# Nineteen constant matmuls ahead of the first transposes, and the fifth projected tile taken out of PSUM by VectorE

## The chip, the cores and the metric

The kernel runs on one core of a Trainium2 chip. The metric is the device time of one execution in microseconds (us). TensorE multiplies matrices into PSUM; VectorE (DVE in the profile), ScalarE (ACT) and GpSimd (POOL) do the elementwise work and take results out of PSUM; SyncE (SP) issues the DMAs.

## The reference

The input is x, 2048 tokens of 512 numbers. With xn = layernorm(x), the result is x + s * g, where s is a dilated local attention and g a gated MLP, both on xn:

```python
def _A_ref(x, wqkv, wo):              # H = 32 heads of 16, W = 8 neighbours, dilation 2
    q, k, v = (x @ wqkv) split into heads
    idx = pos[:, None] - arange(8)[None, :] * 2          # positions before 0 are masked
    attn = softmax(einsum("bhsd,bhswd->bhsw", q, k[idx]) * Dh ** -0.5)
    o = einsum("bhsw,bhswd->bhsd", attn, v[idx])
    return o @ wo
def _B_ref(x, w1, b1, w2, b2):        # 512 -> 1376 -> 512
    y = layernorm(x)
    return gelu(y @ w1 + b1) @ w2 + b2
xn = layernorm(x)
return x + _A_ref(xn, wqkv, wo) * silu(_B_ref(xn, w1, b1, w2, b2))
```

## The kernel before

The tokens are split by parity into two halves of 1024 (c = 0 and 1, since the dilation is 2), each in eight tiles of 128 tokens; the heads are split into four blocks of 128 columns. A "unit" is one half with one block of heads: eight units in all. For each unit `qkv` multiplies the eight normalised and transposed tiles (`yT`) with that block's q, k and v weights (`wq`), twelve matmuls to a tile: all operands are kept as a high and a low float16 part, so a product is high x high, low x high and high x low, four matmuls of 384 columns each. The tile stands in one PSUM buffer of the rings `ps` and `mh` and is then scaled by a per-token factor (`cs`) and written to `U`, by ScalarE (line 824) or by VectorE (line 820). Copies on SP shift the keys and values of the neighbours into place ("halo", line 832), and VectorE does the attention of the unit. The MLP runs over four chunks of 512 tokens and eleven slices of the hidden layer (`mlp1`, line 1111; `mlp2`, line 1158), and the output projection is line 1025.

The first unit (u = 0) stands at the start, while inputs still arrive. `ln0` normalises the tiles in the order 2, 3, 0, 1, 4, 5, 6, 7 (IORD0): statistics (lines 661, 662) and small factors (625, 647) on VectorE, a power on GpSimd (635), the normalised tile on VectorE (697, or 730 in two parts for tile 2, or 665 on ScalarE for tile 4), four transposes on TensorE (704; 738 for tile 2), then the high part by ScalarE (719) and the low part by VectorE (720). Tiles 2 and 3 go another way in this unit: their transposed tile is copied to `L` (741, 708) and multiplied in float32 with the unscaled weights (809). Meanwhile `prep_q` finds the scale of the weights: a sum of squares on ScalarE (578), a sum over the partitions by a matmul with a constant tile `fours` (495, one for each half of the weights), a few tiny steps on VectorE (506, 513, 519, 524), then the high part of the weights by ScalarE (600, four pieces) and the low part by VectorE (602, four pieces). Line 500 is the same sum for the other weights. The last four of a tile's twelve matmuls in this unit read the low parts of the weights, each its own piece, and each waits for that piece of line 602.

Which tile of a unit VectorE takes out of PSUM is listed in `EDVE`, for the first and the second unit; the others go to ScalarE.

The order on each engine is written by a planner (class `Plan`). Every operation has an estimated duration, a priority and its dependencies; `order` places them one after another by estimated time, and each engine then runs its list in that order, without reordering. `place` estimates DMAs from a rate and a start; `SEEDS` perturbs the estimated durations before the order is made, so other seeds give another order throughout the kernel. "Constant matmuls" are matmuls of `fours` with itself into a buffer that nobody reads (line 1260). Their priority of 1e9 lets them be placed only where nothing else is ready by the planner's estimate; before, thirty have no dependency at all, and four more wait for the normalised tile 2.

```python
EDVE = ((5, 6, 7), ())
...
    idle = fours
    for n in range(WAKE0 + WAKE):
```

Of the kernel before, what the change touches and what calls it, by code (L numbers as in the profile page):

```python
# [19 lines left out]
P = 128  # L20
# [34 lines left out]
W2LATE = 4  # L55

QDVE = ()
EDVE = ((5, 6, 7), ())

BEFORE_W1 = (0, 1, 4, 5)  # L60

# [34 lines left out]
class Plan:  # L96
# [71 lines left out]
    def start(self):  # L168
        for o in self.ops:
            o.npred, o.ready, o.succs = len(o.preds), 0.0, []  # L170
        for o in self.ops:
            for p in o.preds:
                p.succs.append(o)
        self.free = {o.eng: 0.0 for o in self.ops}
        self.portfree, self.dma, self.landed, self.table = 0.0, 0.0, [], None
        self.held = False

    def earliest(self, o):
# [7 lines left out]
    def place(self, o, t):  # L186

        if o.eng == "sp":
            if not o.nbytes:
                return t  # L190
            self.free["sp"] = t + o.issue
            self.dma = max(self.dma, t + o.issue + 0.3)
            self.dma += o.nbytes / (o.rate if self.dma > SLOW else 265e3)
            end = self.dma + o.tail
            self.landed.append(end)
            return end
        end = t + o.dur
        if o.nbytes:
            self.free[o.eng] = end
            self.dma = max(self.dma, end + 0.3) + o.nbytes / o.rate  # L200
            return self.dma + o.tail
        if o.eng == "act" and o.table is not None and o.table != self.table:
            end += 1.3
            self.table = o.table
        if o.hold is not None:
            self.held = o.hold
        self.free[o.eng] = end
        if o.port:

            self.portfree = end - (0.25 if o.eng == "pool" else 0.0)  # L210
        return end + LAT[o.eng]
# [123 lines left out]
    def issue(self):  # L335
        self.lengths = [(o.dur, o.tail, o.rate) for o in self.ops]
        best = min(SEEDS, key=lambda seeds: self.judge(seeds)[0]) if len(SEEDS) > 1 else SEEDS[0]
        order = self.judge(best, 0)[1]
# [3 lines left out]

SEEDS = ((186, 978148, 510074, 22688, 804624, 962081, 422754, 653699, 424371, 432252),)

LAT = {"dve": 0.12, "act": 0.14, "pool": 0.07, "pe": 0.06}
MARGIN = {"pe": 0.2, "dve": 0.15, "act": 0.05}  # L350

SLOW = 5.5

QUEUE = 8

# [3 lines left out]

PTOT = 0.5  # L360

WAKE = 4
WAKE0 = 30
PS1 = 0.72

QHI = 4
# [25 lines left out]
def tile_mixer(ctx, tc, a_x, a_wqkv, a_wo, b_w1, b_b1, b_w2, out):  # L392
    nc = tc.nc
    pl = Plan()
# [384 lines left out]
    def qkv(c, hb, u):  # L779
# [11 lines left out]
        left = pl.users([(x, ub, j) for x in "qkv" for j in range(NI)])  # L791
        on_dve = EDVE[u] if u < 2 else ()
        for n, i in enumerate(IORD if u else IORD0):
# [461 lines left out]
    zero_halo(0)  # L1255
    zero_halo(1)
    idle = fours
    for n in range(WAKE0 + WAKE):
        b = R_z[0].new()
        pl.add("pe", 0.2 if n < 16 else 0.1, lambda b=b: nc.tensor.matmul(b.t[:, 0:2 * P], idle[:, 0:P], idle, start=True,  # L1260
                                                       stop=True), [("yd", 2)] if n >= WAKE0 else [], [b], prio=1e9)
    pl.prio = 0.6
    qkv(0, 0, 0)
    pl.prio = PWQ1
# [196 lines left out]
```

## Time and profile before

| | |
|---|---|
| median of 3 runs | 413.49 us (413.47 to 413.73) |
| the profiled execution: its own time | 413.5 us |
| its span, first to last instruction | 411.7 us |
| instructions | 5576 |

A page of the profile shows one execution. Its parts are the busy time of each engine, the span in 40 slices, the DMA queues, the chain of work that ended last (followed back from the last instruction to what released it), the costliest groups of instructions, and the DMA issues. A timeline row gives start and length in us, engine, line, operation, what is written and read, the shape, how often (x), and in brackets the idle time before it and what ended it. Lengths of matmuls are modelled and overlap the next; their pitch is read from start to start.

### The profile page before, as it was taken

The page shows a single profiled execution, that of the slowest core. Times are in us where ns is not written, and L with a number is a line of the kernel's source. Part 1 is how long each engine was busy: PE and PEld are TensorE (multiplying, and loading weights), DVE is VectorE, ACT ScalarE, POOL GpSimd, SP SyncE. Part 2 cuts the span into 40 slices and gives each one's busy share as a digit, 9 for nine tenths or more (in the row PEclk, how much of TensorE's full clock was granted, in tenths as well). Part 3 has the DMA queues.
Part 4 walks back from the last instruction along what each step waited for, and adds up shares of the span by engine and source line. Part 5 has one row for each costly group of instructions (what it writes and reads, how often), then busy time and mean ns, then how long its engine had stood idle before and what let it go on. Part 6 is the DMA issues. An engine that isn't in the chain of part 4 may idle for free.

```text
span 411.7 us, 5576 instructions
## 1 busy us (share of the span) xinstructions
PE 407.0 (99%) x2098; PEld 208.8 (51%) x2098; DVE 387.3 (94%) x372; ACT 224.5 (55%) x359; POOL 114.2 (28%) x160
## 2 busy tenths in 40 slices
PE   8999999999999999999999999999999999999996
PEld 6666444446544554456444644445655554444443
DVE  5999999999999999999999979999989999999965
ACT  4999999876569377432675261126311492234500
POOL 7620542052912250015101500054036500250022
PEclk9999999999999999999999999999999999999999
DMA  8963350500343448400740070302063367008034
GB/s 291 415 259 90 98 198 0 204 2 1 90 111 120 105 128 160 81 0 2 175 144 27 2 164 27 104 0 74 4 192 112 102 205 156 2 0 256 2 79 176
DMA packets 42666, 44.83 MB, mean 109 GB/s; under 512 B 27496, under 2 KB 27936, under 8 KB 42128
## 3 DMA queue, kind: packets, MB, share of 16 engines
q1 hardware_dynamic: 42640, 44.49, 36.4%
q8 instruction: 16, 0.26, 0.2%
q14 instruction: 10, 0.08, 0.1%
HBM read 23.53 MB, written 7.34 MB: 75 GB/s over the span
## 4 chain that ended last, share of the span: by engine, by line
PE 99%; DVE 0%; issue 0%
PE z L1158 28%; PE ps L802 27%; PE mh L1111 26%; PE ps L1025 6%; PE mh L802 2%; PE z L1025 2%; PE z L1260 1%; PE mh L1025 1%; PE ps L1111 1%; PE z L704 1%; PE mh L809 1%; PE ps L809 1%; PE z L738 0%; DVE U L1081 0%; DVE U L1084 0%; PE mh L1142 0%
## 5 line engine op out<-in xcount | busy, mean ns | idle before, releaser
L1111 PE MATMUL mh<-yT,w 128*128 128x512 f16 (+1 forms) x504 | 115.5, 379 | 0.0
L802 PE MATMUL ps<-wq,yT 128*128 128x384 f16 x684 | 114.5, 326 | 0.0
L1158 PE MATMUL z<-w,h 128*128 128x512 f16 x480 | 111.0, 379 | 0.0
L802 PEld LDWEIGHTS <-yT 128*128 128x128 f16 x744 | 72.4, 98 | 48.6 <-issue 0.2
L1111 PEld LDWEIGHTS <-w 128*128 128x128 f16 (+1 forms) x528 | 52.9, 100 | 60.9
L1128 ACT ACTIVATE mh<-mh,b1T,hsc 128x512 f32<-128x512 f32 (+1 forms) x42 | 31.5, 749 | 85.1 <-PE mh L1111 84.8
L1158 PEld LDWEIGHTS <-h 128*128 128x128 f16 x480 | 46.9, 98 | 55.7
L872 DVE TENSOR_TENSOR prod<-U 128x2048 f32<-128x2048 f32 x32 | 72.9, 2282 | 1.4 <-DMA U<-U 1.0
L876 DVE TENSOR_REDUCE L<-prod 128x128 f32<-128x2048 f32 x32 | 73.1, 2285 | 0.8
L824 ACT ACTIVATE U<-ps,cs 128x384 f32<-128x384 f32 x57 | 32.9, 579 | 60.4 <-PE ps L802 58.5
L945 DVE TENSOR_TENSOR prod<-L,U 128x2048 f32<-128x2048 f32 x25 | 60.1, 2423 | 0.2
L976 POOL COPY gate<-prod 1x1 f32<-1x1 f32 x24 | 4.2, 173 | 157.6 <-DVE prod L872 157.6
L977 POOL TENSOR_TENSOR prod<-prod 128x1024 f32<-128x1024 f32 x14 | 32.9, 2349 | 0.0
L1025 PEld LDWEIGHTS <-oT 128*128 128x128 f16 x204 | 19.8, 98 | 21.7
L936 DVE TENSOR_TENSOR prod<-prod,prod 128x2048 f32<-128x2048 f32 x13 | 29.7, 2283 | 0.0
L1025 PE MATMUL ps<-wo,oT 128*128 128x512 f16 (+1 forms) x132 | 28.5, 367 | 0.0
L1136 DVE SCALAR_TENSOR_TENSOR h<-mh,hsc,h 128x512 f16<-128x512 f32 x36 | 26.4, 735 | 0.6 <-ACT h L1132 0.6
L1132 ACT ACTIVATE h<-mh,hsc 128x512 f16<-128x512 f32 x38 | 26.0, 683 | 0.8
L977 POOL TENSOR_TENSOR prod<-prod,oT 128x1024 f32<-128x1024 f32 x3 | 10.0, 3324 | 41.7 <-DVE prod L936 41.7
L1018 POOL TENSOR_TENSOR f<-f,f 128x512 f32<-128x512 f32 x4 | 10.6, 2639 | 22.6 <-DMA U<-U 18.9
L977 POOL TENSOR_TENSOR prod<-prod,prod 128x1024 f32<-128x1024 f32 x7 | 16.4, 2350 | 0.0
L1018 POOL TENSOR_TENSOR U<-U,f 128x512 f32<-128x512 f32 x4 | 5.5, 1374 | 34.3 <-DVE U L1090 34.3
(184 smaller groups left out, 411.1 us busy)
## 6 DMA issues: line engine op xcount, KB each, us to landing
f<-in_A_x_dram SPq DMA_DIRECT2D x31, 256.0 KB, 3.3
U<-U SPq DMA_DIRECT2D x16, 392.0 KB, 4.1
gd<-f SPq DMA_DIRECT2D x12, 256.0 KB, 2.8
oT<-in_B_w_dram SPq DMA_DIRECT2D x2, 1024.0 KB, 9.1
yT<-in_B_w_dram SPq DMA_DIRECT2D x2, 1024.0 KB
f<-gd SPq DMA_DIRECT2D x8, 256.0 KB, 3.8
out_dram<-f SPq DMA_DIRECT2D x8, 256.0 KB, 3.0
out_dram<-U SPq DMA_DIRECT2D x7, 256.0 KB, 2.0
```

The source lines that it names most:

```text
L802: nc.tensor.matmul(b.t[:, 0:384], y[:, s, k, o:o + P], wq[:, hb, t, k], start=(n == 0), stop=(n == 11))
L824: act(384, lambda i=i, b=b: nc.scalar.activation(U3[:, i:i + 31:15, :], b.t[:, 0:384].rearrange("p (t e) -> p t e", t=3), AF.Identity, sca ...
L872: first = dve(2048, lambda p2=p2, g=g: nc.vector.tensor_tensor(p2(), q, slots(Ut, KH, 2 * g), op=ALU.mult), qk + [("kh", ub, 0), ("kh", ub ...
L876: first.then = dve(2048, lambda pr=pr, g=g: nc.vector.tensor_reduce(L3()[:, 2 * g:2 * g + 2], pr.t.rearrange("p (r f d) -> p r f d", r=2, ...
L936: dve(n, lambda: nc.vector.tensor_tensor(d(), a(), b(), op=ALU.add), keys, [dkey])
L945: dve(2048, lambda: nc.vector.tensor_tensor(dst().rearrange("p (r f d) -> p r f d", r=2, d=DH), L3()[:, 2 * g:2 * g + 2].rearrange("p r (f ...
L977: nc.gpsimd.tensor_tensor(d, d, y(), op=ALU.add)
L1025: nc.tensor.matmul(b.t[:, cols], oT[:, hb, i // 4, s, i % 4], wo[:, t, hb, cols], start=(hb == 0 and n == 0), stop=(hb == last and n == 2))
L1111: nc.tensor.matmul(b.t[0:M], w1[:, s, k, f * P:f * P + M], yT[ch][:, t, k], start=(n == 0), stop=(n == 11))
L1128: act(512, lambda: nc.scalar.activation(b.t[0:M], b.t[0:M], AF.Gelu_apprx_tanh, bias=b1T[0:M, f:f + 1], scale=hsc[0:M, 1:2]), [b, ("b1T",) ...
L1136: dve(512, lambda: nc.vector.scalar_tensor_tensor(lo()[0:M], b.t[0:M], hsc[0:M, 2:3], hi()[0:M], op0=ALU.mult, op1=ALU.subtract), [b, hk], ...
L1158: nc.tensor.matmul(z.t, hl[s][0:K, t * P:(t + 1) * P], w2[0:K, w, f], start=(f == 0 and n == 0), stop=(f == NF - 1 and n == 2))
```

## The change

The constant matmuls become nineteen, none of which waits for anything. The first has priority 0 and an estimate of 1.333 us, the others 0.153 us each at the old priority. VectorE takes tiles 4, 6 and 7 of the first unit out of PSUM, in place of 5, 6 and 7. The planner's estimate of the DMAs starts at 2.24 us and has no slower first stretch, and the seeds are others.

```diff
-EDVE = ((5, 6, 7), ())
+EDVE = ((4, 6, 7), ())
...
-        self.portfree, self.dma, self.landed, self.table = 0.0, 0.0, [], None
+        self.portfree, self.dma, self.landed, self.table = 0.0, FIRST, [], None
...
-            self.dma += o.nbytes / (o.rate if self.dma > SLOW else 265e3)
+            self.dma += o.nbytes / o.rate
...
-SEEDS = ((186, 978148, ...),)
+SEEDS = ((500165, 389854, ...),)
...
-SLOW = 5.5
+FIRST = 2.24
...
-WAKE = 4
-WAKE0 = 30
+WAKE = 19
...
-    for n in range(WAKE0 + WAKE):
+    for n in range(WAKE):
         b = R_z[0].new()
-        pl.add("pe", 0.2 if n < 16 else 0.1, lambda b=b: nc.tensor.matmul(b.t[:, 0:2 * P], idle[:, 0:P], idle, start=True,
-                                                       stop=True), [("yd", 2)] if n >= WAKE0 else [], [b], prio=1e9)
+        pl.add("pe", 0.153 + (1.18 if n == 0 else 0.0), lambda b=b: nc.tensor.matmul(
+            b.t[:, 0:2 * P], idle[:, 0:P], idle, start=True, stop=True), [], [b], prio=1e9 if n else 0.0)
```

In the order that the planner then writes, the engines' lists differ in these places (lines as before the change). TensorE: nineteen constant matmuls in place of 23 at the start, and none of the two, two and five that stood further on in the first unit, nor of the two behind the last product; the first transpose of line 738 stands ahead of the first sum of line 495, and the second sum of line 495 ahead of the first transposes of line 704. Later, one group of three of line 1111 and six of line 1158 trade places with their neighbours. VectorE: line 820 for tile 4 stands where one line 720 stood, one line 647 two places further up, and two pairs of neighbours later on are swapped. ScalarE: line 824 for tile 5 in place of the one for tile 4; around the first MLP steps line 1128 and line 542 trade places; a SiLU (line 1174) joins the three ahead of it, which saves two loads of a function table. GpSimd: one pair swapped. SP: three pairs of neighbours swapped. The instructions are otherwise the same.

More of the change, by code (lines that the diff above doesn't have):

```diff
@@ L341, in issue @@
             o.fn()
-SEEDS = ((186, 978148, 510074, 22688, 804624, 962081, 422754, 653699, 424371, 432252),)
+SEEDS = ((500165, 389854, 427978, 647943, 394648, 289068, 629827, 866434, 58414, 290909, 969430, 478841,
+          326988, 34468, 300308, 816254, 306888, 41293, 60788, 308971, 890734, 237800, 376148, 36800, 231455,
+          772755, 355690, 761464),)
 LAT = {"dve": 0.12, "act": 0.14, "pool": 0.07, "pe": 0.06}
 MARGIN = {"pe": 0.2, "dve": 0.15, "act": 0.05}
-SLOW = 5.5
+FIRST = 2.24
 QUEUE = 8
```

## The prediction

> **What bounds the kernel now.** I read the page first, then the timeline of TensorE over the first 30 us, then VectorE and ScalarE over the same stretch, and last a few places late in the run where the new order moves something.
>
> The page:
> ```profile
> span 411.7 us, 5576 instructions
> PE 407.0 (99%) x2098; PEld 208.8 (51%) x2098; DVE 387.3 (94%) x372; ACT 224.5 (55%) x359; POOL 114.2 (28%) x160
> PE 99%; DVE 0%; issue 0%
> ```
> The chain that ended last is TensorE from end to end. Its useful work is the same before and after, so only two things can move the time: constant matmuls that stand between useful ones, and stalls. The first 24 us of TensorE (start, length, line, count; a length is modelled and overlaps the next row, so I read the pitch from start to start):
> ```profile
> 1.18 5.09 PE L1260 MATMUL z<-fours 128*128 128x256 bf16 x23 [1.18 <-DVE s L1315]
> 6.06 0.21 PE L495 MATMUL z<-s,fours 128*128 128x1 bf16 x1
> 6.13 1.08 PE L738 MATMUL z<-ident,f 128*128 128x128 f32 x4
> 7.02 2.18 PE L809 MATMUL ps<-prod,L 128*128 128x384 f32 x6
> 9.03 0.60 PE L704 MATMUL z<-ident,f 128*128 128x128 f32 x4
> 9.47 0.17 PE L495 MATMUL z<-s,fours 128*128 128x1 bf16 x1
> ...
> 13.43 0.38 PE L1260 MATMUL z<-fours 128*128 128x256 bf16 x2
> 13.65 0.60 PE L704 MATMUL z<-ident,f 128*128 128x128 f32 x4
> 14.09 0.81 PE L802 MATMUL ps<-wq,yT 128*128 128x384 f16 x4
> 14.73 0.38 PE L1260 MATMUL z<-fours 128*128 128x256 bf16 x2
> 14.95 0.81 PE L802 MATMUL mh<-wq,yT 128*128 128x384 f16 x4
> ...
> 17.78 0.71 PE L1260 MATMUL z<-fours 128*128 128x256 bf16 x5
> 18.32 0.81 PE L802 MATMUL ps<-wq,yT 128*128 128x384 f16 x4
> 18.97 0.81 PE L802 MATMUL mh<-wq,yT 128*128 128x384 f16 x4
> 19.62 2.11 PE L802 MATMUL ps<-wq,yT 128*128 128x384 f16 x12
> 21.57 0.60 PE L704 MATMUL z<-ident,f 128*128 128x128 f32 x4
> ...
> 23.98 0.60 PE L704 MATMUL z<-ident,f 128*128 128x128 f32 x4
> ```
> Two things are to be seen. The opening 23 constant matmuls have a pitch of (6.06-1.18)/23 = 0.212 us, the five at 17.78 one of 0.108: TensorE runs at half speed at first. The four transposes of 6.13 still take 0.22 each, the six passes of 7.02 take 0.335, so full speed comes at about 7.2. (The page's granted clock shows full speed throughout; this slowness is in the pitch alone.) And from 13.43 on, rows follow each other without a hole: TensorE works on, also through the nine constant matmuls at 13.43, 14.73 and 17.78, which take 9 x 0.108 = 0.98 us of the path.
>
> Who would be late without them? VectorE and ScalarE there:
> ```profile
> 5.34 0.34 DVE L730 TENSOR_SCALAR f<-prod,lw,lw 128x128 f32<-128x128 f32 x1 [0.69 <-POOL lw L635]
> 6.32 0.69 DVE L661 BATCH_NORM_STATS2 bn<-prod 128x6 f32<-128x512 f32 x1 [0.24 <-DMA prod<-in_A_x_dram]
> 8.10 0.55 DVE L697 TENSOR_SCALAR f<-prod,lw,lw 128x512 f32<-128x512 f32 x1 [0.63 <-POOL lw L635]
> 9.51 0.15 DVE L625 TENSOR_SCALAR lw<-lw 128x1 f32<-128x1 f32 x1
> 9.71 0.16 DVE L506 TENSOR_SCALAR ssq<-z 128x1 f32<-128x1 f32 x1
> 14.22 1.38 DVE L720 TENSOR_TENSOR yT<-z,yT 128x512 f16<-128x512 f32 x2
> 16.04 2.20 DVE L602 SCALAR_TENSOR_TENSOR wq<-prod,qsc,wq 128x384 f16<-128x384 f32 x4
> 19.16 1.28 DVE L720 TENSOR_TENSOR yT<-z,yT 128x512 f16<-128x512 f32 x2
> 23.09 0.54 DVE L697 TENSOR_SCALAR f<-prod,lw,lw 128x512 f32<-128x512 f32 x1
> 14.29 0.58 ACT L719 CAST yT<-z 128x512 f16<-128x512 f32 x1
> ```
> After the wait at 8.10 VectorE shows none up to 25 us. Its start is held by a DMA (6.32) and GpSimd (8.10), neither of which the change touches, so VectorE's chain is what limits how much of the 0.98 us comes back.
>
> **The change part by part.**
>
> *Four of the opening 23 go, and the first transpose passes ahead of L495.* The 19 that are left end at 1.18 + 19 x 0.212 = 5.21. The first quarter of the normalised tile is there at 5.34 + 0.34 = 5.68, so the first transpose runs at about 5.74, not 6.13. The other three need the rest of that tile; at L697's 0.55 us for 512 columns its 384 take about 0.41, so they run from about 6.13, as the first did before, and with 3 x 0.212 L809 starts at 6.77, not 7.02. Of these 0.25 us the half speed until 7.2 takes half: L809 ends at 8.9, not 9.03.
>
> *L495 ahead of L704.* L495 now runs at 8.9, not 9.47. L506 on VectorE waited for it: it stood at 9.71, while L625 at 9.51 allows 9.58. VectorE gains 0.13 us.
>
> *The nine in between go.* L704 at 13.65 moves up by 0.1 from the start and 0.22 from its two constant matmuls, to 13.33; its input is ready before that. The products of 14.95 need the cast of 14.29, which ends at 14.87; as the cast itself waits for L704, but also for ScalarE's work before it, I give it 0.2: they start at 14.70. The 2.83 us of work from 14.95 to 17.78 then end at 17.53. Next come four products that each wait for one of the four L602. That quartet ends at 16.04 + 2.20 = 18.24; it gains the 0.13, and 0.10 more because the pair of L720 at 14.22 has in it 0.10 that the like pair at 19.16 has not (a wait for that same cast), and the new order puts a 0.07 us step there. So the last L602 ends at 18.01, the fourth product runs at 18.06 and ends at 18.22, in place of 18.97: 0.75 us ahead. With two groups of 0.65 (18.32 to 18.97, and the like) tile 4's first third then ends at 19.52, but its second third needs the first L720 of 19.16, which ends at 19.84 - 0.23 = 19.61: a stall of 0.14. Lead: 0.61 us. That wait is what comes late next.
>
> *VectorE takes tile 4 out of PSUM, ScalarE tile 5.* One L820 of 0.61 us stands earlier on VectorE, and one L720 of a tile that is not wanted yet moves behind L697 in exchange: the transposes of 23.98 need the L697 of 23.09 (ends 23.63, new 23.4), and would start at 23.37. That is even, to 0.05. ScalarE's 0.6 us only move by a few places; neither buffer is written again before the next unit, so I cost it at nothing. Cover gone, it would be 0.05 to 0.1.
>
> *The rest of the order.* The new seeds and DMA start move seven groups on TensorE, all of the same work. On SP's queue three pairs of neighbours change places, among them a halo copy that now stands behind a store and waits for its SiLU; the reader of that copy is several of VectorE's 2.3 us instructions further on. On GpSimd two short steps swap. Both cost nothing under that cover. Two places on TensorE are tight. First, at 215 us four products move ahead of a 2.6 us block, and their buffer must have been read by a SiLU that now comes directly behind the other three, into an output buffer that a store still reads:
> ```profile
> 211.05 6.11 SPq L1177 DMA_DIRECT2D gd<-f  x4
> DMA to landing us min/median/max: 2.0/2.8/3.1
> 215.20 2.75 PE L1111 MATMUL mh<-yT,w 128*128 128x512 f16 x12
> ```
> The store issued at 211.05 lands at 213.05 to 214.15, the SiLU of 0.69 ends by 214.9, before 215.2: no stall, and two table loads of 1.28 us on ScalarE vanish beside TensorE. Second:
> ```profile
> 331.36 1.04 ACT L824 ACTIVATE U<-ps,cs 128x384 f32<-128x384 f32 x2
> 331.99 2.11 PE L802 MATMUL ps<-wq,yT 128*128 128x384 f16 x12
> ```
> Here L802 starts as soon as ScalarE has emptied its buffer (331.36 + 0.58), so a lead of TensorE lasts only if the others have it too. They have:
> ```profile
> 29.86 0.16 DVE L504 TENSOR_REDUCE s<-z 128x1 f32<-128x4 f32 x1 [0.20 <-PE z L500]
> 249.13 0.75 DVE L1039 SCALAR_TENSOR_TENSOR f<-ps,osc,f 128x512 f32<-128x512 f32 x1 [0.25 <-PE ps L1025]
> ```
> VectorE waited for TensorE at 29.86 and at 249.13, so it takes over the lead. The two constant matmuls at the end of TensorE's list stand behind the last useful one and cost nothing now.
>
> *Sum.* The profiled execution took 413.5 us for a span of 411.7; the median of the runs is 413.49, so I take them as one. 413.5 - 0.6 = **412.9 us**. A measurement of this kernel can tell about 0.2% (0.83 us) from no change, so this counts as within it.
>
> **The rivals.**
>
> *Slower: full speed comes late.* Before, it took 6.0 us of unbroken matmuls (1.18 to 7.2). After, TensorE stands still from 5.21 to 5.74 and from about 6.0 to 6.13. If that hole starts the count anew, full speed comes 6.0 us after 5.74, at 11.7: 4.5 us longer at half speed, 2.25 us lost, of which the stall of 0.14 and the lead of 0.61 are to be taken: +1.5, **415.0 us**. It turns slower by over 0.2% when full speed comes after about 10.3. Against it: the hole is 0.6 us in 6. For it: the constant matmuls are the only work TensorE has then, and no run shows how much of a hole is borne. 18 in 100.
>
> [...]
>
> *Faster: VectorE comes up too.* If VectorE's waits between 8 and 24 us are larger than its rows show, nothing holds TensorE, and the whole 0.98 and the 0.1 ahead of them are gained: **412.4 us**. For it: VectorE stands only 0.5 us behind at 19.6. Against: no row shows an idle VectorE there. 18 in 100.
>
> *The lead is lost.* A new stall at one of the seven moved groups, or at 331.99 if VectorE does not follow, eats it: 413.1 to 413.9, **413.4 us**; at worst the nine only covered waits, and the change does nothing. For it: margins of 0.05 us. Against: 300 us of rows without a hole. 12 in 100.
>
> **How the numbers follow.** 52 in 100 for the forecast (412.6 to 413.1, by 0.1 to 0.25 us on the terms of the walk), 18, 18 and 12 for the rivals. The range takes in the forecast, the faster case and the lost lead, 412.3 to 413.9, and leaves out the 18 of the slow one. Faster by over 0.2% (under 412.67): 18 and 5 from the forecast's edge, 0.23. Slower: 0.18. Within: 0.59.
>
> **What would show it.** Right: one row of 19 constant matmuls from 1.18, a hole before the first L738 at 5.7, the first L809 at 6.8 with a pitch of 0.33 from 7.2 on, L802 of tile 4 at 18.9, its L704 (now 21.57) at about 20.96, and from there every row 0.6 us earlier. Wrong: L809 still at a pitch of 0.64 at 9 us; L506 after 9.7; a last L602 that ends after 18.1; holes on TensorE around 215, 307 or 332 us.

## The result, and the profile after

The changed kernel took 412.57 us (median of 21 runs, 412.32 to 414.36); the kernel before, run beside it, 413.32 us (21 runs, 412.84 to 414.06). The ratio is 0.9986, with a 95% interval of 0.998 to 0.9991: 0.58 us of 413.3, between 0.37 and 0.83 (the two medians are 0.75 apart). The interval doesn't reach 1, but the gain is within the 0.2% that the prediction counts as no change; the forecast was 412.9 us and a gain of 0.6. The profiled execution took 412.75 us (before: 413.5).

The page of the changed kernel; all its line numbers are one higher than before:

```profile
span 410.9 us, 5543 instructions
PE 405.8 (99%) x2083; PEld 206.9 (50%) x2083; DVE 387.4 (94%) x372; ACT 222.4 (54%) x357; POOL 114.7 (28%) x160
PE 97%; DVE 1%; DMA 1%; ACT 0%; issue 0%; POOL 0%; ACTq 0%
```

TensorE has 15 instructions fewer. Its share of the chain that ended last fell from 99% to 97%: where constant matmuls stood, a few short waits show now. TensorE's timeline (start, length, line, count) tells which:

```profile
1.18 4.24 PE L1261 MATMUL z<-fours 128*128 128x256 bf16 x19 [1.18 <-DVE s L1316]
5.46 0.47 PE L739 MATMUL z<-ident,f 128*128 128x128 f32 x1
6.55 2.38 PE L810 MATMUL ps<-prod,L 128*128 128x384 f32 x6
8.76 0.17 PE L496 MATMUL z<-s,fours 128*128 128x1 bf16 x1
...
13.66 0.81 PE L803 MATMUL ps<-wq,yT 128*128 128x384 f16 x4
14.60 0.82 PE L803 MATMUL mh<-wq,yT 128*128 128x384 f16 x4
...
17.43 0.81 PE L803 MATMUL ps<-wq,yT 128*128 128x384 f16 x4
18.08 0.81 PE L803 MATMUL mh<-wq,yT 128*128 128x384 f16 x4
18.73 2.25 PE L803 MATMUL ps<-wq,yT 128*128 128x384 f16 x12
20.81 0.60 PE L705 MATMUL z<-ident,f 128*128 128x128 f32 x4
...
23.22 0.65 PE L705 MATMUL z<-ident,f 128*128 128x128 f32 x4
```

The transposes at 21.57 before now start at 20.81, a lead of 0.76 us, and those at 23.98 at 23.22: the lead is kept. Four products take 0.65 from start to start without a wait, so the hole ahead of 14.60 is 14.60 - 13.66 - 0.65 = 0.29; twelve take 1.96, so the row at 18.73 holds a wait of 20.81 - 18.73 - 1.96 = 0.12. The transposes of 23.22 take 0.05 longer than their fellows. Together 0.46 us of waits stand where 0.98 us of constant matmuls stood, and 0.52 came back there.

VectorE, then ScalarE, in the same stretch of the changed kernel (in brackets the idle time before a row, and what ended it):

```profile
3.21 0.69 DVE L662 BATCH_NORM_STATS2 bn<-prod 128x6 f32<-128x512 f32 x1 [2.07 <-DMA prod<-in_A_x_dram]
5.71 0.69 DVE L662 BATCH_NORM_STATS2 bn<-prod 128x6 f32<-128x512 f32 x1
8.89 0.15 DVE L626 TENSOR_SCALAR lw<-lw 128x1 f32<-128x1 f32 x1
9.00 0.16 DVE L507 TENSOR_SCALAR ssq<-z 128x1 f32<-128x1 f32 x1
14.57 0.69 DVE L721 TENSOR_TENSOR yT<-z,yT 128x512 f16<-128x512 f32 x1 [0.31 <-ACT yT L720]
15.64 2.20 DVE L603 SCALAR_TENSOR_TENSOR wq<-prod,qsc,wq 128x384 f16<-128x384 f32 x4
18.76 1.28 DVE L721 TENSOR_TENSOR yT<-z,yT 128x512 f16<-128x512 f32 x2
```

```profile
13.96 0.58 ACT L720 CAST yT<-z 128x512 f16<-128x512 f32 x1
```

Two things are to be seen. The statistics of the second tile start at 5.71 and wait for no DMA; before they started at 6.32, held by one. VectorE so stood 0.6 us further on in this execution, which is no work of the change: in the twelve profiles of this case these statistics start anywhere from 5.71 to 6.76, in both orders. And VectorE now waits itself, 0.31 us at 14.57, for the cast of 13.96, the same one that TensorE's hole at 14.60 waits for. The last of L603 ends at 15.64 + 2.20 = 17.84, and the products of 17.43 and 18.08 show no wait.

### The profile page after: what moved, and what is told of

It is laid out like the page before. It is cut to its first block, busy times and chain, and to the rows that moved or that the text cites. A ratio compares the mean times of both kernels' runs of the same rounds, so it can differ in the third digit from the quotient of the medians.

```text
span 410.9 us, 5543 instructions
## 1 busy us (share of the span) xinstructions
PE 405.8 (99%) x2083; PEld 206.9 (50%) x2083; DVE 387.4 (94%) x372; ACT 222.4 (54%) x357; POOL 114.7 (28%) x160
## 4 chain that ended last, share of the span: by engine, by line
PE 97%; DVE 1%; DMA 1%; ACT 0%; issue 0%; POOL 0%; ACTq 0%
PE z L1159 28%; PE ps L803 27%; PE mh L1112 26%; PE ps L1026 6%; PE mh L803 2%; PE z L1026 2%; PE mh L1026 1%; PE ps L1112 1%; PE mh L810 1%; PE ps L810 1%; PE z L705 1%; DMA prod<-in_A_x_dram 1%; PE z L739 0%; DVE U L1082 0%; DVE U L1085 0%; DVE bn L662 0%
```

## The experiments

Each was timed beside the kernel before on its chip, and its ratio is to that. The experiments were timed in three sets, in which the kernel before took 413.44 us (the first four runs below, up to the nine put back), 413.22 (the own buffer and the opening count) and 413.31 (the last two), so medians of different sets compare only to some 0.2 us. Where one only adds or leaves out constant matmuls, the computation is the same.

**The nine in between, alone.** The kernel before in its own order, without the nine constant matmuls at 13.43, 14.73 and 17.78 and the two at the end.

```diff
         for t, o in order:
+            if o in self.wake:
+                n += 1
+                if n > 23:
+                    continue
             o.fn()
```

> The kernel before in its own order, but the nine constant matmuls at 13.43, 14.73 and 17.78 (and the two behind the last product) are left out; the 23 opening ones stay. Theory (they stood on TensorE's path, VectorE limits how much comes back): the first unit's tile 4 is stalled by VectorE's L720, lead 0.4 us, time about 413.0, faster than the kernel before by 0.3 to 0.5. Rival 'they only covered waits': no change within 0.1. Rival 'all of it comes back': 0.98 faster.

413.13 us (11 runs, 412.62 to 413.69), ratio 0.9994, 0.9986 to 1.0003: a gain of some 0.25 that the interval doesn't tell from nothing, so the times alone decide neither for the expected 0.3 to 0.5 nor for the rival of no change. TensorE's timeline, with lines six higher than before:

```profile
17.23 0.96 PE L808 MATMUL ps<-wq,yT 128*128 128x384 f16 x4
18.03 0.81 PE L808 MATMUL mh<-wq,yT 128*128 128x384 f16 x4
18.68 2.28 PE L808 MATMUL ps<-wq,yT 128*128 128x384 f16 x12
20.79 0.60 PE L710 MATMUL z<-ident,f 128*128 128x128 f32 x4
...
23.26 0.66 PE L710 MATMUL z<-ident,f 128*128 128x128 f32 x4
```

The profiled execution has nearly the lead of the changed kernel, but it owes some of it to its start (the row of L710 that began at 9.03 before is at 8.62). Its waits are larger: 0.22 ahead of the products that follow 14.0, 0.15 ahead of the last product that waits for VectorE's quartet (at 17.55), 0.15 in the row at 18.68, and 0.11 about 23.2, together 0.63 of the 0.98.

**The four at the opening, alone.** The kernel before in its own order with 19 opening constants instead of 23; the nine stay (`if n <= 4: continue` in the same place).

> The kernel before in its own order with 19 opening constant matmuls in place of 23, the nine later ones kept. Theory: L495 comes 0.1 to 0.5 us earlier, but TensorE still works through the nine, so at most 0.1 to 0.2 us faster. Rival 'a hole in the opening delays full speed': passes of L809 at a pitch of 0.64 for longer and a time 0.5 to 1.5 us slower.

413.34 us (12 runs, 412.94 to 415.04), ratio 1.0007, 0.9996 to 1.0017. Ten runs are like the kernel before (412.94 to 414.06), two took 414.96 and 415.04, and the profile caught the first of these. TensorE's timeline of it, behind the nineteen constants:

```profile
5.55 0.16 PE L501 MATMUL z<-s,fours 128*128 128x1 bf16 x1
5.88 1.29 PE L744 MATMUL z<-ident,f 128*128 128x128 f32 x4 [0.17 <-DVE f L736]
6.97 3.68 PE L815 MATMUL ps<-prod,L 128*128 128x384 f32 x6
10.49 0.60 PE L710 MATMUL z<-ident,f 128*128 128x128 f32 x4
...
23.03 0.60 PE L710 MATMUL z<-ident,f 128*128 128x128 f32 x4
```

The six passes start 0.05 earlier than before and take 3.52 to the next row instead of 2.01: half speed went on until about 10.2 (the passes are 0.64 apart, the last 0.32), and all that follows is 1.46 us later (23.03 against 21.57). This is the slower rival of the prediction, seen in the profiled run and, by its time alone, in a second of the twelve.

**Both, in the order of before.** All fifteen left out (`if n <= 4 or n > 23: continue`).

> The kernel before in its own order with all fifteen constant matmuls left out (19 at the start and no other): what is left to the changed kernel is the order alone (L495 later, tile 5 and not 4 on VectorE, the later moves). Theory: 0.5 to 0.7 us faster than before, so the order is worth 0.1 to 0.2. Rival 'the new order does it': 0.2 or less faster than before.

412.91 us (11 runs, 412.57 to 413.75), ratio 0.9993, 0.9984 to 1.0001. The rows:

```profile
18.73 2.28 PE L808 MATMUL ps<-wq,yT 128*128 128x384 f16 x12
20.84 0.60 PE L710 MATMUL z<-ident,f 128*128 128x128 f32 x4
...
23.32 0.66 PE L710 MATMUL z<-ident,f 128*128 128x128 f32 x4
```

At 20.84 it is 0.03 behind the changed kernel, at 23.32 it is 0.10 behind, with a wait of 0.15 in the row at 18.73 and 0.11 at the last one. By the profiles the new order and tile 4's change of engine so bring 0.1 us more. The times don't show that part: the ratios of the changed kernel are 0.9986 and, in a second set further down, 0.9995, on both sides of this one. Nor do they decide between the expected 0.5 to 0.7 and the rival of 0.2 or less: the gain is 0.3 by the ratio and 0.53 by the medians.

**The nine put back.** The changed kernel with constants at the places where the nine stood.

```diff
         for t, o in order:
+            if o.eng == "pe":
+                for _ in range(self.extra.get(k, 0)):
+                    self.wakeup()
+                k += 1
             o.fn()
...
+    pl.extra = {34: 2, 36: 2, 41: 5}
+    wk = R_z[0].tiles[0]
+    pl.wakeup = lambda: nc.tensor.matmul(wk[:, 0:2 * P], idle[:, 0:P], idle, start=True, stop=True)
```

> The changed kernel with nine constant matmuls put back at the same three places (2, 2 and 5). Theory: TensorE works through them without a hole, the lead at 20 us falls from 0.76 to about 0.1 to 0.2, time 0.1 to 0.2 under the kernel before. Rival 'they cost nothing, the new order brings it': as fast as the changed kernel, 0.7 faster than before.

414.11 us (11 runs, 413.1 to 414.47), ratio 1.0015, 1.0006 to 1.0023: slower than both kernels. The transposes of 21.57 stand at 21.33, so the nine do cost about what was expected there. The rest was lost elsewhere, at 215 us. ScalarE there:

```profile
211.25 1.27 ACT L1180 ACTIVATE f<-z,zsc 128x512 f32<-128x512 f32 x2
215.32 0.69 ACT L1180 ACTIVATE f<-z,zsc 128x512 f32<-128x512 f32 x1 [2.80 <-DMA gd<-f]
```

TensorE:

```profile
213.01 2.10 PE L1164 MATMUL z<-w,h 128*128 128x512 f16 x9
216.05 0.81 PE L1164 MATMUL z<-w,h 128*128 128x512 f16 x3 [0.94 <-ACT f L1180]
```

SP's queue, and of the stores' line the time from issue to landing:

```profile
210.81 5.54 SPq L1183 DMA_DIRECT2D gd<-f  x4
DMA to landing us min/median/max: 2.0/2.9/4.6
```

The fourth SiLU waits until 215.32 for a store issued at 210.81 to have read its buffer, 4.5 us after the issue; TensorE then stands still for 0.94 us. In the changed kernel's profile the same SiLU (ScalarE, first) waited 0.39 and TensorE (second) not at all:

```profile
212.44 0.69 ACT L1175 ACTIVATE f<-z,zsc 128x512 f32<-128x512 f32 x1 [0.39 <-DMA gd<-f]
```

```profile
212.54 2.75 PE L1159 MATMUL z<-w,h 128*128 128x512 f16 x12
```

**That SiLU with a buffer of its own.** The changed kernel, in which this SiLU writes to a part of `yT` that is no longer read, so that it waits for no store.

```diff
                 g = R_f.new()
+                if ch == 1 and t == 3:
+                    pl.spare = g
...
+        self.spare.ring.tiles.append(self.own)
+        self.spare.slot = len(self.spare.ring.tiles) - 1
...
+    pl.own = f32v(yT[0], 4)[:, 0]
```

> The changed kernel, but the SiLU that follows the other three at 212 us writes into a buffer of its own (part of the finished first half's yT), so it does not wait for a store to land. Order and work are the same. Theory (that wait reaches TensorE only when the store lands late): median 412.4 to 412.6, as the changed kernel, with fewer executions above 413. Rival 'the wait is hidden anyway': the same median and the same spread up to 414. Rival 'it costs every time': 0.3 or more faster than the changed kernel.

412.71 us (12 runs), ratio 0.9988, 0.998 to 0.9997. Eleven runs lie between 412.45 and 412.80, one at 414.43. The usual execution doesn't gain (expected were 412.4 to 412.6), as the wait at 215 us costs it nothing. The runs at 413.3 to 413.7, of which the changed kernel has two in 21, are missing here, but twelve runs are too few to say that the buffer took them away.

**Both: own buffer, nine put back.**

> The changed kernel with the nine constant matmuls back and that SiLU's own buffer. Theory: without the stall at 214.7 us the nine cost 0.5 to 0.7 against the changed kernel: 413.0 to 413.2, 0.2 to 0.4 under the kernel before. Rival 'the nine themselves made it slow': 413.9 to 414.2 again.

413.22 us (12 runs, 412.89 to 414.99; nine of them up to 413.70, three at 414.81 to 414.99), ratio 1.0005, 0.9993 to 1.0016. The expected 0.2 to 0.4 under the kernel before is missed: that took 413.22 too. TensorE's timeline:

```profile
12.97 0.38 PE L1429 MATMUL z<-fours 128*128 128x256 bf16 x2
...
14.28 0.38 PE L1429 MATMUL z<-fours 128*128 128x256 bf16 x2
...
17.32 0.71 PE L1429 MATMUL z<-fours 128*128 128x256 bf16 x5
17.86 0.81 PE L810 MATMUL ps<-wq,yT 128*128 128x384 f16 x4
...
19.16 2.11 PE L810 MATMUL ps<-wq,yT 128*128 128x384 f16 x12
21.11 0.60 PE L712 MATMUL z<-ident,f 128*128 128x128 f32 x4
```

Each row follows the last without a hole, as all of them do from 13 to 23 us. Between this and the kernel without the nine, of the same set, lie 413.22 - 412.71 = 0.51 us (0.40 if the three late runs here and the one there are left aside), and 0.98 - 0.46 is 0.52: the nine cost about their length less the waits that they covered. The run with the old buffer stood 0.67 above the kernel before of its set, this one 0.00: that difference is the stall at 215 us, which took 0.94 in its row and, by their times, not all of its runs.

**The opening count.** The changed kernel with 8 opening constants, and with 23 (four more, issued behind the nineteen: `pl.extra = {19: 4}`).

```diff
             if o in self.wake:
                 n += 1
+                if n > 8:
+                    continue
```

> The changed kernel with 8 opening constant matmuls in place of 19, all else as it is: TensorE stands still from 2.9 to about 5.5 us. Theory 'a hole delays full speed, by the length of the hole and by chance of its place': in most executions L809 at a pitch of 0.6 until 9 to 11 us and a time of 414 to 415. Rival 'full speed comes by the clock, whatever stands there': 412.6, as the changed kernel.

> The changed kernel with 23 opening constant matmuls in place of 19, ahead of the first transpose. Theory: the first transposes come up to 0.4 us later, L809 0.1 to 0.25 later, and as the waits at 14.5 and 19.5 us take in most of that, the median is 0 to 0.2 above the changed kernel; no executions with a late full speed. Rival 'the four were on the path in full': 0.4 above it.

Eight: 414.07 us (9 runs, 413.91 to 414.97), ratio 1.0023, 1.0013 to 1.0032. TensorE's timeline:

```profile
1.18 1.89 PE L1267 MATMUL z<-fours 128*128 128x256 bf16 x8 [1.18 <-DVE s L1322]
5.83 0.47 PE L745 MATMUL z<-ident,f 128*128 128x128 f32 x1 [2.77 <-DVE f L737]
6.92 3.38 PE L816 MATMUL ps<-prod,L 128*128 128x384 f32 x6
10.13 0.17 PE L502 MATMUL z<-s,fours 128*128 128x1 bf16 x1
```

With a hole of 2.77 us the half speed goes on until about 9.5 us (four passes 0.64 apart, the last two 0.33 and 0.32). By their times it came about so late, or later, in all nine runs. With 23: 412.71 us (11 runs, 412.56 to 413.2), ratio 0.9987, 0.9979 to 0.9996. The median is that of the nineteen with the own buffer in the same set (412.71), and no run is late, as expected.

**Both spreads taken away, and the changed kernel once more.** 23 opening constants and the own buffer together, and the changed kernel unaltered, on one chip.

> The changed kernel with both things that moved its runs apart taken away: 23 opening constants instead of 19, and the SiLU of the place at 215 us writing into a buffer of its own. Theory (the opening count decides whether full speed ever comes late, the store's landing decides the 1.1 us at 215 us, and neither touches the usual execution): median 412.5 to 412.8, the same as the changed kernel to 0.1, and no run above 413.2. Rival (the late executions have another cause, for example the first x tile's landing): one or two runs in twelve at 413.5 to 415 as with the own buffer alone, median the same.

> The changed kernel once more, unaltered, beside the one with 23 opening constants and the own buffer. Theory: median 412.5 to 412.7 with one or two of its runs between 413.2 and 414.5 (a late store at 215 us, 1.1 us, or a late full speed, 1.4 us). Rival (its outliers belonged to one chip): all runs between 412.3 and 412.9.

The first: 412.78 us (11 runs, 412.51 to 413.29), ratio 0.9989, 0.998 to 0.9997. The changed kernel: 412.82 us (12 runs, 412.29 to 414.52), ratio 0.9995, 0.9985 to 1.0006. That is above the expected 412.5 to 412.7, and four of its runs lie above 413.2 (413.29, 413.38, 414.48 and 414.52), more than expected. The medians are alike, so no version is faster than the changed kernel in its usual execution; the one with 23 and the own buffer only lacks runs above 413.3. Its two at 413.28 and 413.29 miss the expected limit of 413.2, and the profile caught the first. VectorE, then TensorE:

```profile
6.69 0.69 DVE L669 BATCH_NORM_STATS2 bn<-prod 128x6 f32<-128x512 f32 x1 [0.61 <-DMA prod<-in_A_x_dram]
```

```profile
9.08 0.66 PE L712 MATMUL z<-ident,f 128*128 128x128 f32 x4 [0.28 <-DVE f L705]
```

The second tile's statistics wait 0.61 for their DMA, TensorE then waits 0.28 for the tile, and the transposes of 23.98 stand at 23.76: a lead of 0.22 where the changed kernel's first profile has 0.76 (23.22). So a third thing moves runs apart, the landing of the second tile of x, and here it made an execution of 413.28 with neither a late store nor a late full speed. The profile with 23 and the old buffer (413.15 us) shows the same wait (0.52, the statistics at 6.58). The profile of the changed kernel's second set begins:

```profile
1.18 3.67 PE L1261 MATMUL z<-fours 128*128 128x256 bf16 x19 [1.18 <-DVE s L1316]
5.53 0.33 PE L739 MATMUL z<-ident,f 128*128 128x128 f32 x1 [0.69 <-DVE f L731]
6.31 2.12 PE L810 MATMUL ps<-prod,L 128*128 128x384 f32 x6
```

The nineteen take 3.67 here against 4.24 in the first profile, so full speed came among them (at a pitch of 0.213 and then 0.108, after some 14 of them, at about 4.2 us), and it outlasted the hole of 0.69. The lead at 23.98 is 1.15 here, and this execution took 412.34 us.

## Why the prediction was right

**The opening.** Nineteen constants, a first transpose at 5.46 and a first L810 at 6.55, forecast for 5.74 and 6.77. Both are early because the first tile's statistics started at 3.21 instead of 3.49. Full speed came at about 7.1 (the first of the six passes takes 0.60, the second 0.32), against 7.2.

**L495 ahead.** The sum stands at 8.76 and L507 at 9.00, right behind L626: the step of 0.20 between the two rows of VectorE became 0.11. The gain is 0.09, forecast 0.13; in the second profile the step is 0.07 (8.96 to 9.03) and the gain 0.13.

**The nine.** Forecast were a next wait of 0.14 for VectorE's L720 in tile 4's second third and an even last row; they measure 0.12 and 0.05. The products forecast for 14.70 stand at 14.60, with the cast as their bound, as argued; this hole is 0.19 to 0.29 in all eight profiles without the nine. The term that came out otherwise is the end of the quartet of L602: forecast 18.01, because "VectorE's chain is what limits how much of the 0.98 us comes back"; it ended at 17.84 and held nothing. In that execution the limit was the cast on ScalarE, and the lead 0.76 instead of 0.61. The walk itself was sound: from the start of the second tile's statistics to the end of the quartet it is 11.92 us before (6.32 to 18.24), and 11.66 to 11.68 in four profiles of the new order (own buffer, 23 constants, both, and the changed kernel's second), 0.25 less where 0.23 was forecast. What was off is where this stretch starts, 5.71 instead of 6.32: 0.28 of it because the first tile landed earlier (3.21 instead of 3.49), 0.33 because the second did. Both landings differ between executions, and the forecast was walked along one of them. In the order of before without the nine, the same quartet does hold TensorE, by the 0.15 at 17.55, and in the changed kernel's second profile by 0.08 at 17.26. So the limit that the prediction named is real, and either can come last.

**The swap of tiles 4 and 5, the two at the end, 331.99.** Costed at nothing. No wait on TensorE over 0.05 us shows behind 23.3 us in the changed kernel, and its last useful product starts 0.76 earlier (406.94 against 407.70), the lead of 20.81. The other profiles say the same of all that stands behind 24 us: except for the nine put back, the time of each differs from that of before by what its transposes of 23.98 lead or lag, to 0.07 us (1.15 and 412.34, 0.76 and 412.75, 0.22 and 413.28, -1.46 and 414.96 against 413.5). The nine put back lead by 0.24 there and are 0.81 slower, so that one execution lost 1.05 behind it. VectorE does take the lead over: its row that began at 249.13 stands at 248.42.

**The place at 215 us** is where the argument failed although the number held. It let the store land 2.0 to 3.1 us after its issue, the spread of the one profile, and found 0.3 us to spare. The nine put back show a landing at 4.5 us and 0.94 us of stall, where the two profiles of the changed kernel show 2.1 from issue to SiLU at that place (210.34 to 212.44, and 209.94 to 212.05), and the one with 23 constants the same wait of 0.39 before the SiLU. Elsewhere in the changed kernel's first profile stores of this line took up to 4.2, and in its second the median was 4.1. The changed kernel's runs at 413.3 to 413.7 may have had the stall or a late second tile, as the profile at 413.28 had; none of them was profiled, and that stays open. Why the store is late in most runs with the nine put back and in few of the changed kernel isn't settled.

**The slower rival** is real and was priced too high. Half speed did go on after a hole in the opening, not for 6.0 us counted anew (11.7, 415.0 us) but until 10.2, and with eight constants and a hole of 2.77 us until about 9.5: no run shows that a hole starts the count anew. The late runs of the changed kernel took 414.36, 414.48 and 414.52, 0.5 to 0.6 under the rival's 415.0. The moment differs between runs of one kernel: it is 7.1 and 4.2 us in the two profiles of the changed kernel. Of the 80 runs with 19 opening constants, those with the nine put back and the old buffer aside, 9 were over 1.5 us above their kernel's median; of the 33 with 23 opening constants none, and none of the 111 runs of the kernel before, which has 23 too. One of the nine was profiled, the others are taken as such by their times. The chance of 18 in 100 was for every execution; it is about one execution in nine.

**The faster rival**, VectorE coming up too, came half true: VectorE had time to spare, and the cast on ScalarE held TensorE instead, 0.29 us. 412.57 us is just below the forecast's own range (412.6 to 413.1) and nearer to this rival's 412.4 than to 412.9, the second set's 412.82 in it. That the ratio gives 0.58 for a forecast of 0.6 is in part luck: the two profiles of the changed kernel lead by 0.76 and 1.15.

## What to carry to other kernels

Filler work on the bounding engine costs its length less the waits behind it that it covers: here nine constants of 0.98 us cost 0.4 to 0.5, because 0.46 us of waits came out from under them. Walk the chain of every engine that stands within some tenths of a microsecond, and don't let one execution's DMA landing decide which of them is the limit. A margin against a store's landing needs the largest landing of several executions (here 3.1, 4.2 and 4.6 us in three profiles); and filler that keeps an engine busy until full speed is judged by its late runs (here 9 of 80 with nineteen constants, none of 33 with 23), which the median doesn't show.

## What the runs showed of the hardware

Full speed after the start came at about 4.2, 7.1 and 10.2 us in executions that all open with nineteen constant matmuls, while the mean granted clock that their profiles show is 1.0, 0.999 and 1.0. The earliest is the profile of the nine put back: 0.11 instead of 0.21 from matmul to matmul from about 4.0 us on, 2.8 us after the first one, and full speed then outlasted a hole of 1.10. The late one (the four at the opening, alone) and the run with all fifteen left out open with the same instructions, and their row of six passes begins 0.24 us apart:

```profile
5.89 0.96 PE L744 MATMUL z<-ident,f 128*128 128x128 f32 x4 [0.17 <-DVE f L736]
6.73 2.20 PE L815 MATMUL ps<-prod,L 128*128 128x384 f32 x6
```

Here, without the four and the nine, full speed was there by the first passes: the four transposes take 0.84 to the next row (1.09 in the late run), and the six passes 2.04 (3.52), to 8.77. The holes were like those of the late run: 0.17 before the transposes in both. So neither the count nor the hole alone decides, and what does isn't shown.

The same kind of store, 256 KB to `gd`, landed 2.0 to 3.1 us after its issue in the profile before, 2.3 to 4.2 in the changed kernel's first and 2.0 to 4.6 in that of the nine put back; the medians were 2.8, 3.7 and 2.9, and 4.1 in the changed kernel's second.
